# A third raw weight buffer, alternating channel groups and an earlier first norm in a one-core SSM and feed-forward kernel

## The chip, the cores and the metric

The kernel runs on one core of one Trainium2 chip. The metric is the device time of one execution in microseconds (us); a profiled execution also has a span, from its first to its last instruction. TensorE (PE) multiplies matrices into PSUM, VectorE (DVE) and ScalarE (ACT) do elementwise work, GpSimd (POOL) does some elementwise work and issues transfers, SyncE (SP) only issues transfers. Each engine takes its instructions in order.

## The reference

One layer: an adaptive layer norm, a state-space convolution over 2048 positions, a second adaptive norm and a dense feed-forward part. All is float32. Cut to what matters:

```python
mod = (silu(c) @ w_mod).reshape(1, 6, 1, 576)
sa, ca, ga, sb, cb, gb = (mod[:, i] for i in range(6))

def ssm(h):                                   # h: 2048 x 576 channels
    dt = exp(log_dt); A = -exp(log_A_real) + 1j * A_imag        # 576 x 128
    C = (C_real + 1j * C_imag) * dt[:, None]
    K = 2 * einsum("dn,dnl->dl", C, exp((A * dt[:, None])[:, :, None] * arange(2048))).real
    return causal_convolution(h, K) + h * D_skip   # in the reference by FFTs of length 4096

h = layernorm(x) * (1 + ca) + sa
x = x + ga * ssm(h)
h = layernorm(x) * (1 + cb) + sb
out = x + gb * (relu(h @ w1) @ w2)            # w1: 576 x 4608, w2: 4608 x 576
```

## The kernel before

The 2048 positions are four blocks of 512. For each block the kernel makes a convolution (`conv`, with s the block) and a feed-forward part (`ffn`). The matrix products of the feed-forward part have their operands split into a high and a low part in a faster float format (`fp32r`), and three of the four partial products are summed.

**The convolution kernel.** `KGen` builds K from powers: for each of 12 groups of 48 channels (h = 0 to 11) a table `W2` of 32 powers and a table `W1` of 16 start values, so that one small matmul gives values of K. Part of it is made at the start (`first`), and the rest later (`rest`), from tables kept in DRAM. `rest` takes a plan: for each h, which blocks of K are to be made. `load0` loads `W0` and `Z`, `load2` loads `W2`, all on POOL's queue in program order. `rots` turns `W0` by multiplying it with `Z` (four VectorE steps a rotation, lines 464 to 470) into a tile `W1r`, `products` does 96 small matmuls for each half of the group (line 498) and copies the result with ScalarE (line 508) into `ker`; after h = 5 and h = 11 it is stored to DRAM (`kd`). `spread` hands out the rotations of a group between the products of the group before. In block 0 the groups 0 to 5 make three blocks of K (three rotations, 48 columns) and 6 to 11 make one (one rotation, 16 columns).

**The convolution of a block.** `norm1` makes the first norm: eight `bn_stats`, four means and scales (`norms`), and eight VectorE operations into h (lines 914 and 915). A DFT matmul (`transform`, line 831, with ScalarE's evacuation at line 832) is made of h (`mm_U`) and of K (`mm_K`, from a tile `kt` loaded from `kd`), each in two halves p = 0, 1. `spec_U` and `spec_K` finish the spectra on VectorE by butterflies (lines 843 to 859), `product` multiplies and sums spectra of all block pairs (lines 1011 to 1017), `inverse` goes back (line 1038). Then the second norm follows, and five transposes, which give `xh`, `xl` and `xs`, the input of the feed-forward part.

**The feed-forward part.** `ffn` runs over 144 groups g, 36 for each block. A group has 14 matmuls of `first` (line 1311) into `hps`, ScalarE's `hh` (line 1316) and VectorE's `hl` (line 1317), and 14 matmuls of `second` (line 1337) into five accumulators. Its weights come by SyncE as raw tiles `r1` (line 1256) and `r2` (line 1260). ScalarE makes the high parts (`hi1`, line 1276, and `hi2`, line 1286) and in block 0 VectorE makes the low parts (`lo1`, line 1281, and `lo2`, lines 1292 and 1293), which are stored and loaded again in later blocks. There are two `r1` and two `r2` buffers; the loads at the top of group g are those of `r1[g+3]` and `r2[g+2]`.

**The order of the work.** The feed-forward part of block b is laced with the other work of the next block: `gens[b]` is a generator whose yields are costs (a number: so many us of VectorE work; None: a piece of TensorE work; -1: stop this step). `step` is called four times a group and draws from it while the work done is below a target, at most 7.5 units of VectorE work in four steps in block 0, and two pieces of TensorE work in a step. What is left after the 36th group is drained at once. For block 0 the generator is `block0`: `rest` for all 12 groups, then `conv(1)`. A scheduler places the instructions on each engine's queue, earlier program order first, as its own clock finds them ready; what goes through `Kept` stays in program order on its engine. A tile whose slot is still read waits for its readers. All transforms share one PSUM tile (`cps`).

Of the kernel before, what the change touches and what calls it, by code (L numbers as in the profile page):

```python
# [10 lines left out]
F32 = mybir.dt.float32  # L11
# [38 lines left out]
class KGen:  # L50
# [385 lines left out]
    def rest(self, psum, plan):  # L436

        nc, k = self.nc, self.k
        v = nc.vector.tensor_tensor
        hs = list(plan)  # L440
        with ExitStack() as ctx:
            pt = k.pool(ctx, f"kr{len(hs)}", side="right")
            most = used = 16 * max(len(b) for b in plan.values())

            d = Kept(k.tc, nc.gpsimd).dma_start

            def load0(h):
                W0 = pt.tile([P, 16, 2, H], F32, tag="W0", bufs=3, name=f"W0_{h}")
                Z = pt.tile([P, 2, 2, H], F32, tag="Z", bufs=3, name=f"Zr_{h}")
                d(out=W0.rearrange("p a r c -> p (a r c)"), in_=k.W1d[h])  # L450
                d(out=Z.rearrange("p i r c -> p (i r c)"), in_=k.Zd[h])
                return W0, Z

            def load2(h):
                W2 = pt.tile([P, 2, 32, H], F32, tag="W2", bufs=2, name=f"W2r_{h}")
                d(out=W2.rearrange("p r b c -> p (r b c)"), in_=k.W2d[h])
                return W2

            def rot(out, X, Z, i):
                cb = [P, 32, H]  # L460
                flat = "p a r c -> p (a r) c"
                T = pt.tile([P, 16, 2, H], F32, tag="T", name="T")
                zr, zi = (Z[:, i, r].unsqueeze(1).broadcast_to(cb) for r in range(2))
                v(T.rearrange(flat), X.rearrange(flat), zi, op=ALU.mult)
                yield 1.75
                v(out.rearrange(flat), X.rearrange(flat), zr, op=ALU.mult)
                yield 1.75
                v(out[:, :, 0], out[:, :, 0], T[:, :, 1], op=ALU.subtract)
                yield 0.95
                v(out[:, :, 1], out[:, :, 1], T[:, :, 0], op=ALU.add)  # L470
                yield 0.95

            def rots(h, W1, W0, Z):
                blocks = plan[h]
                a = [W1[:, 16 * i : 16 * i + 16] for i in range(len(blocks))]
                if blocks[0] == 1:
                    yield from rot(a[0], W0, Z, 0)
                    if len(blocks) > 1:
                        yield from rot(a[1], W0, Z, 1)
                        yield from rot(a[2], a[0], Z, 1)  # L480
                else:
                    yield from rot(a[0], W0, Z, 1)
                    yield from rot(a[1], a[0], Z, 0)

            ke = {}

            def products(h, W1, W2):
                blocks = plan[h]
                na = 16 * len(blocks)
                if h % 6 == 0:  # L490
                    ke[h // 6] = pt.tile([P, na, 72], F32, tag=f"ke{na}", bufs=1, name=f"ker_{h}")
                for half in range(2):
                    ps = psum.tile([P, 6, na], F32, tag="cps", bufs=1, name="kps")
                    for q in range(6):
                        for dd in range(4):
                            ch = dd * 12 + 6 * half + q
                            for r in range(2):
                                nc.tensor.matmul(  # L498
                                    ps[32 * dd : 32 * dd + 32, q, :],
                                    W2[:, r, :, ch],  # L500
                                    W1[:, :, r, ch],
                                    start=(r == 0),
                                    stop=(r == 1),
                                )
                        if q == 2:
                            yield None
                    q0 = 12 * (h % 6) + 6 * half
                    nc.scalar.activation(
                        ke[h // 6][:, :, q0 : q0 + 6], ps.rearrange("p q a -> p a q"), AF.Copy
                    )  # L510
                    yield None
                if h % 6 == 5:
                    yield -1
                    for i, s in enumerate(blocks):
                        self.store(
                            s, h // 6, ke[h // 6][:, 16 * i : 16 * i + 16].rearrange("p a q -> p (a q)"),
                            nc.sync,
                        )

            nxt = [load0(hs[0])]  # L520
            W2 = load2(hs[0])
            nxt.append(load0(hs[1]))
            yield -1
            prev = iter(())
            for i, h in enumerate(hs):
                W0, Z = nxt.pop(0)
                if i + 2 < len(hs):
                    nxt.append(load0(hs[i + 2]))
                na = 16 * len(plan[h])
                if used + na > most:  # L530
                    all1 = pt.tile([P, most, 2, H], F32, tag="W1", bufs=2, name=f"W1r_{h}")
                    used = 0
                W1 = all1[:, used : used + na]
                used += na
                yield from spread(rots(h, W1, W0, Z), prev, len(plan[h]))
                prev = products(h, W1, W2)
                if i + 1 < len(hs):
                    W2 = load2(hs[i + 1])
            yield from prev
# [11 lines left out]
class Body:  # L551
# [195 lines left out]
    def main(self, ctx, kg, hooks):  # L747
# [10 lines left out]

        def block0():
            self.x2p.append(self.pool(ctx, "x2b"))  # L760
            yield from kg.rest(
                self.cps, {h: (1, 2, 3) if h < 6 else (1,) for h in (6, 0, 7, 1, 8, 2, 9, 3, 10, 4, 5, 11)}
            )
            self.xp.append(self.pool(ctx, "xb"))
            pool(1)
            yield from self.conv(1)

# [134 lines left out]
    def norm1(self, x2, h):  # L902
# [9 lines left out]
        for i in range(4):  # L912
# [2 lines left out]
            f(h[:, i], h[:, i], mv[:, 3:4], self.m["sa"], op0=ALU.mult, op1=ALU.add)  # L915
            yield 1.6

    def conv(self, s):

        nc = self.nc  # L920
        v = self.vec.tensor_tensor
        xp = self.xp[s % 2]
        if s:
            x2 = self.x2p[s % 2].tile([P, 4, D], F32, tag="x2", bufs=1, name=f"x2_{s}")
            self.x2[s] = x2
            Kept(self.tc, nc.gpsimd).dma_start(
                out=x2,
                in_=self.I["x"][s * 512 : (s + 1) * 512, :].rearrange("(m n) d -> m n d", n=4),
            )
        else:  # L930
            x2, h = self.x2[0], self.h0
            self.fcKn, self.gcn = (
                self.cv.tile([P, 4, P], F32, name=n) for n in ("fcKn", "gcn")
            )
            for t, a in zip((self.fcKn, self.gcn), self.I["neg"]):
                nc.gpsimd.dma_start(out=t, in_=a)
# [4 lines left out]

        kt = [kernel_tile(0) if s else self.kt0, None]
        yield -1 if s else "mod"
        if s:
            h = self.spec(f"h_{s}").rearrange("p a b c -> p a (b c)")
        hv = h.rearrange("m n (dd p q) -> m n dd p q", dd=4, p=2)

        def mm_U(p, Z):
# [97 lines left out]
        def back(p, Y):  # L1046
            V = self.spec(f"V_{s}_{p}")
            yield from self.butterfly1(Y, V) if s == 0 and p == 0 else self.butterfly(Y, V, 1)
            Vs.append(V)
# [4 lines left out]
        if s == 0:  # L1054
# [15 lines left out]
            ZK = self.spec("Z")  # L1070
            yield from mm_K(1, ZK)
            self.save(self.Rd[0][0], Ks[0], Kept(self.tc, nc.gpsimd))
        else:
            yield from both(self.norm1(x2, h), mm_K(0, ZK))
            kt[1] = kernel_tile(1)
            ZU = self.spec("Z")
            yield from both(spec_K(0, ZK), mm_U(0, ZU))
# [19 lines left out]
        else:  # L1097
# [2 lines left out]
            Y = self.spec(f"Y_{s}_1")  # L1100
            yield from product(1, Y)
        yield from back(1, Y)
        xh = xp.tile([P, 4, 512], F32R, tag="xh", bufs=1, name=f"xh_{s}")
        xl = xp.tile([P, 4, 512], F32R, tag="xl", bufs=1, name=f"xl_{s}")
        xs = xp.tile([P, 512], F32R, tag="xs", bufs=1, name=f"xs_{s}")
# [138 lines left out]
    def ffn(self, gens):  # L1244
# [11 lines left out]
            queue(g).dma_start(out=r1[g], in_=I["w1"][g % NF])  # L1256

        def load_r2(g):
            r2[g] = ff.tile([P, D], F32, tag="r2", bufs=2, name="r2")
            queue(g + 1).dma_start(out=r2[g], in_=I["w2"][(g % NF) * P : (g % NF) * P + P, :])  # L1260

        def low1(g):
# [118 lines left out]
        yield  # L1381
        load_r2(1)
        load_r1(2)
        prev = None
        for g in range(n + 1):
            if g < n:
                if g + 3 < n:
                    load_r1(g + 3)
                if g + 2 < n:
                    load_r2(g + 2)  # L1390
                for dst, src in late:
                    nc.sync.dma_start(out=dst, in_=src.bitcast(F32))
                late.clear()
# [74 lines left out]
def both(a, b):  # L1468

    while True:  # L1470
        n = 0
        for g in (a, b):
            for w in g:
                n = 1
                yield w
                break
        if not n:
            return
# [62 lines left out]
```

## Time and profile before

| what | us |
|---|---|
| median of three runs | 1353.58 |
| lowest and highest run | 1346.75, 1354.69 |
| the profiled execution, own time | 1347.4 |
| its span | 1345.6 |
| feed-forward block 0 (first group to first group) | 221.6 to 554.1 |
| block 1 | 554.1 to 844 |
| blocks 2 and 3 and the end | 844 to 1345.6 |

The rows quoted below come from the profiled execution. L12 is line 12 of the kernel; "out<-in" names the tiles of an instruction; a wait names the engine and line that ended it. PEld is TensorE's loading of weights, SPq and POOLq are the queues that issue transfers. PEclk is the share of TensorE's full clock that was granted. In the chain of waits each row is a start, a duration, and what the time went to.

### The profile page before, as it was taken

The numbers are of one execution on the slowest core, as the hardware profiler recorded it, in microseconds if no ns is written. First come the engines' busy times: TensorE is split into PE (matmuls) and PEld (weight loads), VectorE is DVE, ScalarE is ACT, GpSimd is POOL, SyncE is SP. The second block draws the span as 40 slices with busy tenths as digits, with TensorE's granted clock in tenths as the row PEclk, the third lists the DMA queues.
The fourth block names the chain that finished last, engine by engine and source line by source line (L and its number), as shares of the span: only waits on it lengthen the run. The fifth ranks groups of instructions, "written<-read, shape, count | busy, mean of one in ns | idle before, by whom it ended". The sixth has DMA issues, their size and how long they took to land.

```text
span 1345.6 us, 26013 instructions
## 1 busy us (share of the span) xinstructions
PE 1232.3 (92%) x10720; PEld 983.7 (73%) x10720; DVE 892.2 (66%) x1324; ACT 496.4 (37%) x863; POOL 162.4 (12%) x260
## 2 busy tenths in 40 slices
PE   4556686999999898999999999999999999999997
PEld 2344565778777686777777887887888888888885
DVE  5989978999986899588458985467996221111112
ACT  5778423222224322622244225433323352323331
POOL 0657411001000000100001000100000000000000
PEclk9658887999999999999999999999999999999998
DMA  8567975788867866898778995877996567666661
GB/s 269 217 240 287 332 269 182 283 306 304 302 237 264 332 224 259 262 409 285 244 275 328 343 364 162 271 223 269 348 393 189 176 178 230 194 196 198 199 186 53
DMA packets 120843, 345.85 MB, mean 257 GB/s; under 512 B 23916, under 2 KB 24212, under 8 KB 109972
## 3 DMA queue, kind: packets, MB, share of 16 engines
q1 hardware_dynamic: 103828, 226.96, 51.2%
q0 software_dynamic: 16384, 115.85, 22.7%
q8 instruction: 84, 1.38, 0.4%
q10 hardware_dynamic: 512, 1.38, 0.4%
q14 instruction: 35, 0.29, 0.1%
HBM read 262.73 MB, written 81.40 MB: 256 GB/s over the span
## 4 chain that ended last, share of the span: by engine, by line
PE 82%; DVE 8%; DMA 4%; issue 3%; ACT 2%; POOL 1%; POOLq 0%; ACTq 0%; SPq 0%; DVEq 0%
PE acc L1337 33%; PE hps L1311 33%; PE kps L498 5%; PE ps_f L831 5%; PE kps L71 2%; PE ps_i L1038 2%; DMA r<-in_w_dram 2%; PE ph L71 1%; DMA Zr<-Zd 1%; DVE T L62 1%; DVE W L62 1%; DVE k L62 1%; PE ps_t L1133 0%; POOL W L68 0%; DMA kt<-kd 0%
## 5 line engine op out<-in xcount | busy, mean ns | idle before, releaser
L1311 PE MATMUL hps<-xh,w 128*128 128x512 f32 x1152 | 394.0, 401 | 0.7 <-ACT xh L47 0.7
L1337 PE MATMUL acc<-w,hh 128*128 128x512 f32 x1152 | 369.3, 401 | 4.2 <-ACT hh L1316 4.2
L1317 DVE SCALAR_TENSOR_TENSOR hl<-hps,hh 128x512 fp32r<-128x512 f32 x144 | 99.0, 688 | 324.5 <-ACT hh L1316 323.8
L1337 PEld LDWEIGHTS acc<-w,hh 128*128 128x128 f32 x1152 | 215.7, 188 | 51.0 <-ACT hh L1316 4.6
L1311 PEld LDWEIGHTS hps<-xh,w 128*128 128x128 f32 x1152 | 216.9, 189 | 48.4 <-ACT xh L47 1.3
L1311 PE MATMUL hps<-xl,w 128*128 128x512 f32 x576 | 230.1, 400 | 0.1
L1337 PE MATMUL acc<-w,hl 128*128 128x512 f32 x576 | 223.2, 399 | 1.3 <-DVE hl L1317 1.3
L1316 ACT ACTIVATE hh<-hps 128x512 fp32r<-128x512 f32 x144 | 86.1, 598 | 303.3 <-PE hps L1311 301.6
L1286 ACT ACTIVATE w<-r 128x576 fp32r<-128x576 f32 x141 | 96.8, 686 | 268.6 <-PE acc L1337 197.3
L1337 PEld LDWEIGHTS acc<-w,hl 128*128 128x128 f32 x576 | 108.0, 188 | 25.6 <-DVE hl L1317 2.5
L1311 PEld LDWEIGHTS hps<-xl,w 128*128 128x128 f32 x576 | 108.7, 189 | 23.9 <-DVE xl L47 0.8
L1276 ACT ACTIVATE w<-r 128x640 fp32r<-128x640 f32 x140 | 102.5, 732 | 24.7 <-DMA r<-in_w_dram 23.3
L1311 PE MATMUL hps<-xs,w 128*128 128x512 f32 x288 | 96.6, 407 | 0.0
L498 PEld LDWEIGHTS kps<-W1r,W2r 128*32 128x32 f32 x3456 | 67.8, 146 | 30.5 <-issue 19.8
L71 PE MATMUL kps<-W,W 128*32 128x16 f32 x2304 | 45.1, 217 | 44.6 <-POOL W L68 29.0
L498 PE MATMUL kps<-W1r,W2r 128*32 128x16 f32 (+2 forms) x3456 | 76.4, 238 | 7.3 <-issue 4.7
L71 PEld LDWEIGHTS kps<-W,W 128*32 128x32 f32 x2304 | 40.4, 150 | 55.7 <-POOL W L68 31.4
L1017 DVE TENSOR_TENSOR Y<-Y,T 128x1152 f32<-128x1152 f32 x60 | 79.3, 1349 | 0.0
L832 ACT ACTIVATE Z<-ps_f 128x288 f32<-128x288 f32 x120 | 48.9, 409 | 69.5 <-PE ps_f L831 68.3
L1455 POOL DMA_DIRECT2D out_dram<-x x16 | 8.7, 545 | 467.0 <-DVE x L1447 464.7
L1311 PEld LDWEIGHTS hps<-xs,w 128*128 128x128 f32 x288 | 53.4, 189 | 11.6 <-DVE xs L1142 0.3
L1337 PE MATMUL acc<-hl,w 128*128 128x512 f32 x144 | 56.9, 395 | 0.0
(230 smaller groups left out, 1565.4 us busy)
## 6 DMA issues: line engine op xcount, KB each, us to landing
r<-in_w_dram SPq DMA_DIRECT2D x144, 320.0 KB, 3.9
r<-in_w_dram SPq DMA_DIRECT2D x144, 288.0 KB, 4.6
w<-L1d SPq DMA_DIRECT2D x108, 320.0 KB, 4.8
w<-L2d SPq DMA_DIRECT2D x108, 288.0 KB, 2.7
W2r<-W2d POOLq DMA_DIRECT2D x18, 1536.0 KB, 8.8
W2d<-W SPq DMA_DIRECT2D x12, 1536.0 KB, 8.6
Ua<-Ud POOLq DMA_DIRECT2D x15, 1152.0 KB, 9.4
W<-W1d POOLq DMA_DIRECT2D x18, 768.0 KB, 10.1
```

What stands on the lines that cost most here:

```text
L62: self.tc.keep_in_program_order(self.nc.vector.tensor_tensor(out, a, b, op=op))
L71: self.tc.keep_in_program_order(self.nc.tensor.matmul(*args, **kw))
L498: nc.tensor.matmul(ps[32 * dd : 32 * dd + 32, q, :], W2[:, r, :, ch], W1[:, :, r, ch], start=(r == 0), stop=(r == 1),)
L831: nc.tensor.matmul(o, fc[:, n2, c, :], src(n2), start=True, stop=True)
L832: ev = nc.scalar.activation(Z[:, n2, c], ps[:, :PC], AF.Copy)
L1017: v(y, y, T, op=op or ALU.add)
L1276: copy(g - 1)(w1[g][:, 0], r1[g], AF.Copy)
L1286: copy(g)(w[:, 0:D], r2[g], AF.Copy)
L1311: nc.tensor.matmul(ps, a, x, start=(i == 0), stop=(i == 13))
L1316: nc.scalar.activation(hh, ps, AF.Relu)
L1317: nc.vector.scalar_tensor_tensor(hl, ps, 0.0, hh, op0=ALU.max, op1=ALU.subtract)
L1337: nc.tensor.matmul(acc[i], a, x, start=(f == 0 and seen[i] == 1), stop=(f == NF - 1 and seen[i] == (3 if i < 4 else 2)),)
```

## The change

Three things are changed.

- `r2` gets a third buffer; the load at the top of group g becomes `r2[g+3]`, and `r2[2]` is loaded ahead of the loop.
- In `rest` the tiles `W1r` were parts of two slots of 48 columns' size. Now there is one slot for each size where the sizes alternate, and two where they don't (block 1). The order of the 12 groups in block 0 becomes 0, 6, 1, 7, 2, 8, 3, 9, 4, 10, 5, 11; it was 6, 0, 7, 1, 8, 2, 9, 3, 10, 4, 5, 11.
- The load of the next block's `x` and `norm1` become a generator `head`. In block 0 it starts at group 5, and one piece of it follows each TensorE piece of `rest`. Its result lies in a pool `hp` of its own, which is closed before the pool `xb` for `xh`, `xl` and `xs` is opened; `xb` is opened at the end of the convolution, where it was opened ahead of it. With h ready, `conv(1)` begins with the transform of U in place of that of K. For blocks 2 and 3 `head` is drawn from inside `conv`, at the places where its parts stood.

```diff
@@ rest
-            most = used = 16 * max(len(b) for b in plan.values())
...
             for i, h in enumerate(hs):
+                if len(hs) == NH and h == 5:
+                    yield "head"
                 W0, Z = nxt.pop(0)
                 if i + 2 < len(hs):
                     nxt.append(load0(hs[i + 2]))
                 na = 16 * len(plan[h])
-                if used + na > most:
-                    all1 = pt.tile([P, most, 2, H], F32, tag="W1", bufs=2, name=f"W1r_{h}")
-                    used = 0
-                W1 = all1[:, used : used + na]
-                used += na
+                bufs = 1 if len(plan[h]) != len(plan[hs[i - 1]]) else 2
+                W1 = pt.tile([P, na, 2, H], F32, tag=f"W1{na}", bufs=bufs, name=f"W1r_{h}")
@@ block0
-            yield from kg.rest(
-                self.cps, {h: (1, 2, 3) if h < 6 else (1,) for h in (6, 0, 7, 1, 8, 2, 9, 3, 10, 4, 5, 11)}
-            )
-            self.xp.append(self.pool(ctx, "xb"))
+            hp = ExitStack()
+            self.hp = self.pool(hp, "hp")
+            plan = {h: (1, 2, 3) if h < 6 else (1,) for h in (0, 6, 1, 7, 2, 8, 3, 9, 4, 10, 5, 11)}
+            head = iter(())
+            for w in kg.rest(self.cps, plan):
+                if w == "head":
+                    head = self.head(1)
+                    continue
+                yield w
+                if w is None:
+                    for x in head:
+                        yield x
+                        break
+            yield from head
+
+            def xb():
+                hp.close()
+                self.xp.append(self.pool(ctx, "xb"))
+
+            self.xb = xb
@@ Body
+    def head(self, s):
+
+        x2 = self.x2p[s % 2].tile([P, 4, D], F32, tag="x2", bufs=1, name=f"x2_{s}")
+        self.x2[s] = x2
+        Kept(self.tc, self.nc.gpsimd).dma_start(
+            out=x2,
+            in_=self.I["x"][s * 512 : (s + 1) * 512, :].rearrange("(m n) d -> m n d", n=4),
+        )
+        yield 0.0
+        if s == 1:
+            self.h1 = self.hp.tile([P, 4, D], F32, name="h_1")
+        else:
+            self.h1 = self.spec(f"h_{s}").rearrange("p a b c -> p a (b c)")
+        yield from self.norm1(x2, self.h1)
@@ conv
+        if s > 1:
+            norm = self.head(s)
+            next(norm)
...
         yield -1 if s else "mod"
+        if s > 1:
+            first_part = next(norm)
...
+        elif s == 1:
+            ZU = self.spec("Z")
+            yield from mm_U(0, ZU)
+            yield from both(spec_U(0, ZU), mm_K(0, ZK))
+            kt[1] = kernel_tile(1)
+            Z1 = self.spec("Z")
+            yield from both(spec_K(0, ZK), mm_U(1, Z1))
+            ZK = self.spec("Z")
+            first[0] = self.load(self.Ud[0][0], "Ua")
+            yield from both(spec_U(1, Z1), mm_K(1, ZK))
         else:
-            yield from both(self.norm1(x2, h), mm_K(0, ZK))
+            yield first_part
+            yield from both(norm, mm_K(0, ZK))
             kt[1] = kernel_tile(1)
             ZU = self.spec("Z")
             yield from both(spec_K(0, ZK), mm_U(0, ZU))
...
         yield from back(1, Y)
+        if s == 1:
+            self.xb()
+        xp = self.xp[s % 2]
@@ ffn
-            r2[g] = ff.tile([P, D], F32, tag="r2", bufs=2, name="r2")
+            r2[g] = ff.tile([P, D], F32, tag="r2", bufs=3, name="r2")
...
         load_r1(2)
+        load_r2(2)
...
-                if g + 2 < n:
-                    load_r2(g + 2)
+                if g + 3 < n:
+                    load_r2(g + 3)
```

More of the change, by code (lines that the diff above doesn't have):

```diff
@@ L921, in conv @@
         v = self.vec.tensor_tensor
-        xp = self.xp[s % 2]
+        if s > 1:
+            norm = self.head(s)
+            next(norm)
         if s:
[L924 to L929, printed above, removed]
+            x2 = self.x2[s]
         else:
@@ L943, in conv @@
         yield -1 if s else "mod"
+        if s > 1:
+            first_part = next(norm)
         if s:
-            h = self.spec(f"h_{s}").rearrange("p a b c -> p a (b c)")
+            h = self.h1
         hv = h.rearrange("m n (dd p q) -> m n dd p q", dd=4, p=2)
```

## The prediction

> **What bounds the kernel now.** I read the page first: the busy shares, then the chain that ended last.
>
> ```profile
> span 1345.6 us, 26013 instructions
> PE 1232.3 (92%) x10720; PEld 983.7 (73%) x10720; DVE 892.2 (66%) x1324; ACT 496.4 (37%) x863; POOL 162.4 (12%) x260
> PE 82%; DVE 8%; DMA 4%; issue 3%; ACT 2%; POOL 1%; POOLq 0%; ACTq 0%; SPq 0%; DVEq 0%
> ```
>
> TensorE carries 82% of the chain. The share is a mean over unlike stages, so the second view is the table of engines by stretch. I cut it where the work of feed-forward block 0 changes: the channel groups of `rest`, their end, the four transforms of the next convolution, its products and inverses; then block 1, then blocks 2 and 3.
>
> ```profile
> core 0: us, PE busy (x) PEld busy (x) DVE busy (x) ACT busy (x) POOL busy (x), PEclk, DMA share, GB/s
> 221.60:390.50 168.90, 163.32 (x2413) 130.12 (x2414) 160.72 (x171) 44.53 (x79) 18.33 (x35) 0.99 0.83 297
> 390.50:425.30 34.80, 34.80 (x498) 28.47 (x496) 17.27 (x42) 9.71 (x20) 1.72 (x2) 1.00 0.82 295
> 425.30:474.10 48.80, 45.05 (x177) 31.98 (x176) 41.81 (x64) 20.72 (x45) 4.93 (x8) 0.97 0.75 271
> 474.10:554.10 80.00, 75.62 (x323) 60.13 (x321) 72.89 (x119) 26.31 (x45) 2.65 (x5) 0.98 0.73 256
> 554.10:844.00 289.90, 286.97 (x2295) 228.04 (x2295) 210.09 (x267) 103.65 (x191) 24.88 (x43) 1.00 0.82 295
> 844.00:1345.00 501.00, 491.70 (x2172) 402.95 (x2170) 201.53 (x287) 164.72 (x281) 16.69 (x30) 0.99 0.69 221
> ```
>
> Two engines are full in block 0: VectorE is busy 160.7 of 168.9 us in the first stretch and 72.9 of 80.0 in the fourth, and TensorE is nearly full too. Only the second stretch is unlike the rest: VectorE works half of it, yet TensorE works all 34.8 us. From 554 us on TensorE is busy 98 to 99% of the time; nothing of this change can win much there. One feed-forward group costs TensorE 28 matmuls:
>
> ```profile
> 412.45 3.17 PE hps L1311 x14
> 415.62 3.17 PE acc L1337 x14
> ```
>
> so 6.34 us is a group's floor. The third view is what TensorE waited for within block 0 (221 to 554 us; line, releaser, total, times, longest; two waits under 1 us follow), the stock from which this change can gain:
>
> ```profile
> PE acc L1337 <- ACT hh L1316: 4.2, 1, 4.2
> PE ps_f L831 <- ACT Z L832: 3.7, 1, 3.7
> PE kps L498 <- issue: 2.9, 2, 1.9
> PE kps L498 <- ACT ker L508: 2.6, 1, 2.6
> ```
>
> That is 13.4 us. Two of the waits are long, and each is followed by a dip of the granted clock (0.97 and 0.98 in their stretches, 1.00 before): 0.03 of 48.8 us and 0.02 of 80.0 us, about 1.5 us apiece. Stock in all: 16.4 us.
>
> **The change part by part.**
>
> *The norm moves into the last channel groups.* Eight statistics and eight scalings leave the head of the convolution.
>
> ```profile
> 402.45 2.97 DVE L880 BATCH_NORM_STATS2 st<-x 128x6 f32<-128x288 f32 x8
> 410.00 0.69 DVE L1317 SCALAR_TENSOR_TENSOR hl<-hps,hh 128x512 fp32r<-128x512 f32 x1 [3.11 <-ACT hh L1316]
> 416.35 0.69 DVE L1317 SCALAR_TENSOR_TENSOR hl<-hps,hh 128x512 fp32r<-128x512 f32 x1 [3.84 <-ACT hh L1316]
> 422.63 0.69 DVE L1317 SCALAR_TENSOR_TENSOR hl<-hps,hh 128x512 fp32r<-128x512 f32 x1 [3.72 <-ACT hh L1316]
> 424.00 1.54 DVE L914 SCALAR_TENSOR_TENSOR h<-x,mv,m_ca 128x576 f32<-128x576 f32 x2
> 425.46 1.54 DVE L915 SCALAR_TENSOR_TENSOR h<-h,mv,m_sa 128x576 f32<-128x576 f32 x2
> ```
>
> The statistics ran in VectorE's slack already. The scalings are two pairs of rows like the last two, 4 x 1.5 = 6 us, and they start at 424.0, after 10.7 us in which VectorE idled and TensorE did not. The obvious hope, 10.7 us, is therefore not to be had: TensorE ran at its floor right there. What moving 6 us away can do is relieve the stretch behind it. There the chain shows this:
>
> ```profile
> 450.25 0.75 DVE w L1281
> 450.99 0.02 issue
> 451.01 7.94 DMA r<-in_w_dram
> ```
>
> Line 1281 is the last reader of a raw `w1` tile; it stood behind a run of butterflies on VectorE, so the reload of that tile (line 1256) went out at 451.01 and landed 7.9 us later; ScalarE, in order, waited for it with an evacuation (line 832) behind, and TensorE waited 3.7 us for that. With 6 us less queued on VectorE line 1281 comes earlier by more than the 3.7 us. I take the wait and its dip as gone: -3.7 - 1.5 = -5.2 us; the ends are 0 and -5.2.
>
> The Trainium skill's page "TensorE: Matmul & The Clock Gate", Part 1, says the clock falls to half after about one idle window of 3.4 us and comes back after one busy window. By that rule each of the two long waits would cost 1.7 us more, instead of the 1.5 I took from the clock column; the sum would be -5.4 in place of -5.2.
>
> The moved norm also takes its `x` load with it, on POOL's queue one group earlier, ahead of the weights of group 11; a load that VectorE now meets inside a full stretch. The issues of raw weights, `x` and `kt` (KB each, median us to landing), and two of the rotations' four steps:
>
> ```profile
> r<-in_w_dram SPq DMA_DIRECT2D x144, 320.0 KB, 3.9
> r<-in_w_dram SPq DMA_DIRECT2D x144, 288.0 KB, 4.6
> x<-in_x_dram POOLq DMA_DIRECT2D x3, 1152.0 KB, 9.2
> kt<-kd POOLq DMA_DIRECT2D x6, 576.0 KB, 8.3
> ```
>
> ```profile
> L464 DVE TENSOR_TENSOR T<-W,Zr 128x1536 f32<-128x1536 f32 x24 | 42.0, 1750 | 8.8 <-DMA Zr<-Zd 8.8
> L468 DVE TENSOR_TENSOR W1r<-W1r,T 128x768 f32<-128x768 f32 x36 | 34.2, 950 | 0.2
> ```
>
> The handing-out puts the first statistic three of group 5's twelve rotation steps behind the load: one of 1.75 and two of 0.95 us, 3.7 us. If it is queued there, VectorE stands up to 9.2 - 3.7 = 5.5 us with group 11's rotations and the `hl` of a group behind it, and TensorE behind those. But 6 us and more of idle VectorE follow, so I take +1, nearer to the slack; ends 0 and +5.5.
>
> *Alternation.* Each group of `rest` already got a tile of its own out of two slots, so group i+2 waited for the products of group i; with one slot for each of the two sizes it still does. Same instructions, same waits (lines 466 on 498). What differs is the order. Group 0 with three rotations now comes first instead of group 6 with one; TensorE gets its first products three rotations later and does feed-forward groups meanwhile. The 2.6 us wait on line 508 lay at these first products, behind a raw load on ScalarE. I take -1.8 of it; ends -2.6 and, if TensorE meets the longer rotation at its first product instead, +2.4, one more wait as long as the longest that VectorE has there:
>
> ```profile
> DVE W1r L466 <- PE kps L498: 6.8, 4, 2.4
> SPq L1260 <- DVE w L1293: 192.6, 29, 15.4
> ACT w L1286 <- DMA r<-in_w_dram: 55.2, 11, 10.0
> ACT w L1276 <- DMA r<-in_w_dram: 20.7, 10, 9.4
> ```
>
> *The third `r2` buffer.* The reload at line 1260 waits for line 1293 (192.6 us in all, SyncE's own idle time). With three buffers the tile loaded in group g still goes into the one that group g's low part has read, so it is issued at the same moment; it only lands one group ahead of need. ScalarE's 55.2 us before line 1286 would go. But line 1276, the raw `w1` with its two buffers as before, is right behind: of the other long wait the chain shows
>
> ```profile
> 507.14 13.03 DMA r<-in_w_dram
> ```
>
> that is `w1` again, landing after 13.0 us where the median is 3.9 to 4.6. The 4.2 us wait on line 1316 lies behind it on ScalarE; so it stays, and I take 0 for the buffer; ends 0 and -5.7 (4.2 and its dip).
>
> *The new order of transforms* (U first, kernel second) is the same 32 transforms of one PSUM tile: cost 0, as long as the second `kt` load stays hidden (rival two).
>
> *The count of steps.* By the handing-out rule (at most 7.5 units of VectorE work in four steps, two pieces of TensorE work in each) I counted the yields of both versions: the generator of block 0 is empty in group 34 before and in group 33 after. Nothing is left over for the drain in either; no term.
>
> Sum: -5.2 + 1 - 1.8 = -6.0 us. The profiled execution took 1347.4 us (span 1345.6), 6 us under the median of the three runs, 1353.58, near the lowest, 1346.75. A difference carries over: 1353.6 - 6.0 = 1347.6 us.
>
> **The rivals.** *One: the whole stock goes.* If less pressure on VectorE brings line 1281 forward everywhere and early `w2` loads free ScalarE, all 16.4 us of the stock fall: 1337.2. For it: both long waits are a raw tile reloaded late. Against: the second lies 90 us behind the norm, amid the transfers of the products, which stay. Chance 0.24.
>
> *Two: slower, by the second kernel tile.* `kt` has one buffer. Before, its reload had two phases (norm or K beside U) before its reader came; now the kernel transform is second and only one phase of eight transforms lies between.
>
> ```profile
> 429.29 0.48 PE ps_f L831 x2
> 430.48 0.55 PE ps_f L831 x2
> 435.25 1.17 POOL L1234 DMA_DIRECT2D kt<-kd  x1 [30.08 <-DMA r<-in_w_dram]
> POOL Rd L822 <- DVE K L859: 17.5, 2, 14.0
> ```
>
> Eight transforms at 1.2 us are 10 us of cover; the load needs 1.2 to issue and 8.3 to land. It decides from half a us on: if POOL, in order, first waits for VectorE to finish a tile that it stores (14.0 us the longest), the load lands up to 14 us late, TensorE stands in order with the feed-forward matmuls behind it, and the clock dips: +14 + 1.5 - 6.0 = +9.5, 1363; without the other gains +15.5, 1369. Against: loads and stores are not kept in program order there, so POOL may take the load first. Chance 0.18. The page "DMA: Bandwidth & Descriptors" of the Trainium skill puts the fixed cost of a transfer at about 2 us; by it this load would be hidden; the 8.3 us row says that under this traffic it lands four times later.
>
> *Three: nothing moves.* The third buffer is issued by the same event, and the late `w1` only shows up at another group: 1353.6. Chance 0.18.
>
> **How the numbers follow.** The forecast has 0.40. About 1% (13.5 us) is what a measurement of this kernel can tell from no change: its three runs lie 0.6% apart. Faster by more needs rival one: 0.24. Slower by more needs rival two without the other gains: 0.12, the rest of its 0.18 lies within. Within 1%: 0.64. The range reaches from 1332, which lies between rival one reckoned from the median (1337) and from the lowest run (1346.75 - 16.4 = 1330), to the middle between rival two's two ends, 1366.
>
> **What would show it.** Right: the scalings of the norm lie before the last products of `rest`, the stretch after them has no wait of TensorE over 3 us at line 831 and a clock of 1.00; the idle time of line 1286 on raw loads falls by most of 55 us while that of line 1276 stays or grows; blocks 1 to 3 are as they were. Wrong: a wait of TensorE or VectorE on `kt` or `x`, or new waits of ScalarE on `w1` loads in front of line 832 or 1316; or a first feed-forward block shorter by over 15 us, which would mean that the late reloads were VectorE's doing throughout.

## The result and the profile after

| | median of 20 runs, us | lowest, highest |
|---|---|---|
| before | 1348.66 | 1346.02, 1354.69 |
| changed | 1350.14 | 1346.08, 1354.43 |

The ratio of changed to before is 1.0004, with a 95% interval from 0.9993 to 1.0016. That is no change: at most 1 us gained or 2 us lost. The forecast was 1347.6 from a base of 1353.58, a ratio of 0.9956, and 0.9956 lies outside the interval. So the time is within the stated range and within 1%, as the likeliest class had it, but the small gain of 6 us is not there. That the forecast in us is only 2.5 us off is luck: the base of three runs was itself 5 us high (over 20 runs the kernel before has 1348.66), and that hides most of the gain that did not come.

In the changed kernel line 1352 is the old 1311 (`hps`), 1378 is 1337 (`acc`), 1357 is 1316 (`hh`), 1317 and 1327 are 1276 and 1286 (the high parts of `w1` and `w2`), 1322 is 1281 (low part of `w1`), 844 and 845 are 831 and 832 (transform and evacuation). The table of engines by stretch of the changed kernel, cut at the first matmul of groups 0, 18, 26, 36 and 72 (columns as in the prediction's table):

```profile
223.30:393.40 170.10, 163.85 (x2413) 128.88 (x2414) 156.81 (x169) 44.97 (x79) 18.54 (x35) 0.99 0.82 295
393.40:471.90 78.50, 78.50 (x672) 59.18 (x671) 63.52 (x108) 30.19 (x65) 6.66 (x10) 1.00 0.83 303
471.90:554.20 82.30, 76.66 (x330) 60.54 (x329) 72.42 (x120) 28.52 (x49) 2.66 (x5) 0.98 0.72 250
554.20:844.50 290.30, 288.03 (x2289) 228.77 (x2288) 209.66 (x266) 101.69 (x187) 24.89 (x43) 0.99 0.83 294
```

and of the kernel before at the same groups, where the prediction's table was cut elsewhere:

```profile
390.50:474.10 83.60, 79.85 (x672) 60.44 (x671) 59.08 (x105) 30.43 (x65) 6.65 (x10) 0.98 0.78 281
554.10:844.10 290.00, 287.07 (x2295) 228.14 (x2295) 210.09 (x267) 103.65 (x191) 24.88 (x43) 1.00 0.82 295
```

Stretch by stretch: the channel groups 170.1 against 168.9 (+1.2), the transforms 78.5 against 83.6 (-5.1), products and inverses 82.3 against 80.0 (+2.3), block 1 +0.3. The sum is -1.3, of a profile whose span is 0.7 us longer in all, 1346.3 us; the part ahead of block 0 was 1.7 us longer in this execution, and the end 0.3. So something was won in the place that the prediction named, and most of it was lost on both sides of it.

TensorE's waits in block 0 of the changed kernel (line, releaser, total, times, longest; five shorter rows follow):

```profile
PE acc L1378 <- ACT hh L1357: 8.0, 3, 4.3
PE hps L1352 <- ACT xh L47: 1.2, 1, 1.2
PE hps L1352 <- DVE w L1322: 1.1, 1, 1.1
PE kps L496 <- PE hps L1352: 1.0, 1, 1.0
```

The 3.7 us wait at the evacuation is gone, and the transforms run at a full granted clock, 1.00 where it was 0.98. In its place there are two more waits at `hh`: 8.0 us in three, where there had been 4.2 in one. All TensorE's waits in block 0 add up to 13.8 us where they had been 14.3. ScalarE's waits for raw tiles show what the third `r2` buffer did:

```profile
ACT w L1317 <- DMA r<-in_w_dram: 55.7, 16, 8.4
ACT w L1327 <- DMA r<-in_w_dram: 0.3, 1, 0.3
```

The wait of 55.2 us at the high part of `w2` is now 0.3, but the one at `w1`, 20.7 before, has become 55.7. ScalarE takes both in order: of 76 us of waiting 56 are left, and they stand one instruction further on.

### The profile page after: what moved, and what is told of

Read it like the earlier page. It is cut to its first block, busy times and chain, and to the rows that moved or that the text cites. A ratio compares the mean times of both kernels' runs of the same rounds, so it can differ in the third digit from the quotient of the medians.

```text
span 1346.3 us, 26017 instructions
## 1 busy us (share of the span) xinstructions
PE 1236.1 (92%) x10720; PEld 983.0 (73%) x10720; DVE 892.7 (66%) x1324; ACT 496.9 (37%) x863; POOL 162.5 (12%) x260
## 4 chain that ended last, share of the span: by engine, by line
PE 82%; DVE 10%; DMA 3%; issue 2%; ACT 1%; POOL 1%; POOLq 0%; ACTq 0%; SPq 0%; DVEq 0%
PE acc L1378 32%; PE hps L1352 32%; PE kps L496 5%; PE ps_f L844 5%; PE kps L71 2%; PE ps_i L1065 2%; PE ph L71 2%; DMA r<-in_w_dram 2%; DVE W1r L464 1%; DVE T L62 1%; DVE T L462 1%; DMA Zr<-Zd 1%; DVE k L62 1%; PE ps_t L1174 1%; POOL W L68 1%
## 5 line engine op out<-in xcount | busy, mean ns | idle before, releaser
L1352 PE MATMUL hps<-xh,w 128*128 128x512 f32 x1152 | 388.2, 397 | 1.2 <-ACT xh L47 1.2
L496 PE MATMUL kps<-W1r,W2r 128*32 128x48 f32 (+2 forms) x3456 | 76.3, 238 | 1.9 <-PE hps L1352 1.0
```

The costliest lines, as they stand in the source:

```text
L496: nc.tensor.matmul(ps[32 * dd : 32 * dd + 32, q, :], W2[:, r, :, ch], W1[:, :, r, ch], start=(r == 0), stop=(r == 1),)
L1352: nc.tensor.matmul(ps, a, x, start=(i == 0), stop=(i == 13))
```

## The experiments

Each is timed in five rounds beside the kernel before on the same chip, and the ratio is to that kernel; the runs were spread over three chips. The short names are those of the expectations. In runs built on the kernel before the lines have other numbers again: 1306 is `hps`, 1311 `hh`, 1332 `acc`, 826 and 827 transform and evacuation, 1271 the high part of `w1`; with both raw buffers 1313 is `hh`, 1314 `hl`, 1334 `acc` and 1273 the high part of `w1`.

**The order alone.** The kernel before with only this:

```diff
-    for h in (6, 0, 7, 1, 8, 2, 9, 3, 10, 4, 5, 11)
+    for h in (0, 6, 1, 7, 2, 8, 3, 9, 4, 10, 5, 11)
-    all1 = pt.tile([P, most, 2, H], F32, tag="W1", bufs=2, name=f"W1r_{h}")
+    W1 = pt.tile([P, na, 2, H], F32, tag=f"W1{na}", bufs=bufs, name=f"W1r_{h}")
```

> The kernel before with the alternating order and the tiles by size alone (two r2 buffers, the norm in its old place, K first). Theory A (the long waits of TensorE are reloads of raw w1 tiles that go out late; the order moves the first of them, the moved norm took away the one in the transforms, nothing else mattered): the wait in the transforms of about 3.7 us stays as before, the start of block 0 is about 1 us longer as in the changed kernel, ratio 1.001 (0.999 to 1.004). Rival B (the alternation itself costs what the norm's move gains, some 4 us): ratio 1.003 or more.

> The order alone once more, since its cost rests on six runs: 1.003 to 1.006 if the order costs what it showed; 0.999 to 1.002 if those runs were unlucky, and then the moved norm gained nothing either.

Measured: 1.0044 (1.0028 to 1.0060), and in the repeat 1.0030 (1.0015 to 1.0045). The order costs 4 to 6 us. The first is Rival B's number and not Theory A's; the repeat lies where the two ranges overlap, and its interval lies above 1 too. Rows of the table by stretch, the channel groups of the first run, then the channel groups and the products of the second:

```profile
225.50:395.70 170.20, 165.34 (x2412) 131.32 (x2413) 159.44 (x170) 44.82 (x79) 18.49 (x35) 0.98 0.81 292
```

```profile
221.70:392.50 170.80, 166.15 (x2413) 131.98 (x2414) 159.95 (x170) 44.12 (x79) 18.49 (x35) 0.97 0.81 291
477.10:558.10 81.00, 76.20 (x323) 60.88 (x322) 73.03 (x119) 26.19 (x45) 2.65 (x5) 0.96 0.73 251
```

The reader is to see TensorE's busy time and the clock: the same 2412 or 2413 matmuls are busy 165.3 and 166.2 us where they were 163.3, and the granted clock is 0.98 and 0.97 for 0.99. In the third stretch it is 0.96 for 0.98. So much of the loss is no idle time at all, but slower matmuls behind the waits. The waits of the second of these runs:

```profile
PE acc L1332 <- ACT hh L1311: 6.8, 3, 4.4
PE ps_f L826 <- ACT Z L827: 3.3, 1, 3.3
PE kps L496 <- issue: 3.1, 2, 2.1
```

With the small ones they add up to no more than before (14.3 us both; in the first run 16.1), but there are three at `hh` instead of one. In the two profiles the clock records show half speed for 13.7 and 17.1 us in block 0, where the kernel before has 6.8 (a dip that lies across the beginning of the block in all three is left out); half of the difference, 3.4 and 5.1 us, is time lost, about the whole price. Of the added dips one lies at 246 us in the first run and two at 243 and 267 us in the second, early in the channel groups, where the kernel before has none; and the dip in the products, 3.4 us long before, is 6.8 in both. By stretch the order alone is longer than before by 1.3 and 1.9 us in the channel groups, 1.4 and 1.0 in the transforms, 0.6 and 1.0 in the products, 0.5 and 0.3 in block 1: 3.8 and 4.2 in all.

The Trainium skill's page "TensorE: Matmul & The Clock Gate", Part 1, says that the clock drops to half after an idle window of 3.4 us, and that the window runs freely. The length agrees: each dip in block 0 is 3.4 us or twice that. But a wait need not fill a window here. In the second run TensorE waited 2.0 us at 240.4, was busy 1.4 of the 3.4 us ahead of 242.6, and the clock dipped there; in the changed kernel a wait of 2.1 us at the same point, 241.9, was followed by no dip, nor was the one of 2.6 us in the kernel before. So which short wait costs a dip as well is partly luck, and waits of equal sum need not cost equal time.

**The small group first.** The same with the order 6, 0, 7, 1, 8, 2, 9, 3, 10, 4, 11, 5, alone and in the changed kernel (where the norm then starts at group 11).

> The kernel before with strict alternation that begins with the small group (6, 0, 7, 1, ... 4, 11, 5) and tiles by size. Theory F (the order alone cost 4 to 8 us because the group of three rotations comes first: TensorE gets no products before group 3, two waits at hh follow): with the small group first the ratio is back at 0.998 to 1.002, products begin in group 2. Rival G (the cost lies at the end of the channel groups or in the tiles by size, not at the beginning): ratio 1.003 to 1.006 as with the large group first.

> The changed kernel with its alternation turned to begin with the small group and to end with a large one (6, 0, ... 4, 11, 5); the norm starts at group 11, again the last but one. Theory F: the moved norm keeps its gain of about 6 us (first to eighth group behind the channel groups 78 us against 83.6 before) and the order costs nothing, ratio 0.994 to 0.997. Rival G: ratio 0.999 to 1.002 as the changed kernel.

Measured: 1.0010 (0.9991 to 1.0028) alone, and 0.9988 (0.9968 to 1.0009) in the changed kernel. Alone it is Theory F's number, and it lies under both runs that began with the large group, although its interval overlaps that of the second. In the changed kernel it is neither: better than 1.0004 by an amount that the intervals don't separate, and not the 0.994 to 0.997 that Theory F gave. This points to the large group at the beginning for most of the order's cost; the two gains don't simply add. (In the one profiled execution of the changed kernel with the small group first, 2 us slower than the median of its runs, no gain is to be seen: the four stretches take 622.9 us against 621.2.)

The clock records of all 14 profiles bear it out. In each of the nine with the large group first a dip of 3.4 us or more begins between 242 and 272 us; in the five that begin with a small group, the kernel before among them, none begins there. The small group first has one wait at `hh` again, 4.1 us in the products, and its first two stretches together take 252.9 us, where the kernel before has 252.5 and the order alone 255.2 and 255.4.

**Without the third `r2` buffer.** The changed kernel with

```diff
-            r2[g] = ff.tile([P, D], F32, tag="r2", bufs=3, name="r2")
+            r2[g] = ff.tile([P, D], F32, tag="r2", bufs=2, name="r2")
-        load_r2(2)
-                if g + 3 < n:
-                    load_r2(g + 3)
+                if g + 2 < n:
+                    load_r2(g + 2)
```

> The changed kernel with two r2 buffers again. Theory A (the third r2 buffer is issued by the same event and only moves ScalarE's idle time from the high part of w2 to that of w1): ratio as the changed kernel, 1.000 (0.998 to 1.003); in block 0 ScalarE idles over 40 us before the high part of w2 on raw loads and under 25 us before that of w1; TensorE has the same waits of 2 to 4.5 us at hh. Rival B (the buffer was worth something that another part gave back): ratio 1.003 or more above the kernel before.

Measured: 0.9998 (0.9985 to 1.0011), the time of the changed kernel. ScalarE waits at the high part of `w2` again, with the rows as expected:

```profile
ACT w L1327 <- DMA r<-in_w_dram: 72.1, 15, 10.0
ACT w L1317 <- DMA r<-in_w_dram: 24.0, 10, 8.2
```

Together 96 us, against 56 with the buffer; and 40 us less of ScalarE's waiting is worth nothing in time. This run is also the order and the moved norm together: against the order alone, the norm (with U ahead of K) gains 0.3 to 0.5%, 4 to 6 us. Its transforms take 77.7 us and its products 83.3:

```profile
393.00:470.70 77.70, 77.70 (x672) 59.26 (x671) 62.64 (x107) 30.29 (x65) 6.64 (x10) 1.00 0.86 314
470.70:554.00 83.30, 77.68 (x330) 60.94 (x329) 73.13 (x121) 28.45 (x49) 2.64 (x5) 0.96 0.68 239
```

**The third `r2` buffer without the norm.** The order with the buffer, the norm in its old place.

> The kernel before with the changed order and a third r2 buffer alone. The buffer is worth nothing without the moved norm too: ratio 1.003 to 1.006 as the order alone; ScalarE's wait moves from the high part of w2 to that of w1. If it is worth something alone: 1.001 or less.

Measured: 1.0014 (0.9998 to 1.0029), between the two answers; the intervals don't decide whether it is worth something alone. The trace does say what it does: the wait at the evacuation is gone here too, and the transforms take 80.4 us where the order alone has 85.0 and 84.6. The reload of raw `w1` behind which that wait lay goes out 10.2 us after the first matmul of group 22; in the kernel before and with the order alone it is 25.8 us.

```profile
391.70:472.10 80.40, 78.82 (x672) 59.49 (x671) 58.73 (x104) 30.56 (x65) 6.11 (x9) 1.00 0.79 289
```

**The third buffer for `r1`.** In the changed kernel in place of the one for `r2`, and on the order alone:

```diff
-            r1[g] = ff.tile([P, 5, P], F32, tag="r1", bufs=2, name="r1")
+            r1[g] = ff.tile([P, 5, P], F32, tag="r1", bufs=3, name="r1")
```

> The changed kernel with the third buffer given to r1 in place of r2. Theory A (raw w1 is what is late): the reload is no longer held by the low part on VectorE, it goes out a group earlier; TensorE's 8.0 us of waits on ScalarE's hh in block 0 fall to under 3 us with the dips of the clock behind them, ratio 0.993 to 0.997. Rival C (the DMA queues are full there, an earlier issue lands no earlier): the waits stay within 2 us of 8 and the ratio within 0.998 to 1.002. Rival D (VectorE's backlog takes over): waits on hh fall but those on hl rise by as much, ratio 0.998 to 1.002.

> The kernel before with the alternating order and a third r1 buffer, the norm in its old place. Theory A: the wait in the transforms goes without the norm's move, since its cause was the reload of raw w1; ratio 0.993 to 0.997, within 0.002 of the run with the norm moved. Rival E (the norm's move is what took it, by VectorE's load): the 3.7 us wait in the transforms stays and the ratio is 0.003 above that run.

Measured: 0.9997 (0.9982 to 1.0012) with the norm moved, a miss for Theory A; its waits at `hh` fell to 3.6 us, but 4.3 us on `hl` came instead, Rival D. On the order alone 0.9982 (0.9969 to 0.9996): a gain of 0.5 to 0.6% over the order alone, though less than Theory A's 0.993 to 0.997, and the transforms at 78.6 us without the norm's move, against Rival E:

```profile
392.80:471.40 78.60, 78.60 (x672) 58.95 (x671) 59.35 (x106) 29.34 (x64) 6.63 (x10) 1.00 0.80 294
```

So the wait in the transforms goes by any one of three edits: the norm moved away, a third `r1` buffer, a third `r2` buffer. Whoever makes two of them wins it once.

**The order of the transforms.** The changed kernel with K first again:

```diff
-            yield from mm_U(0, ZU)
-            yield from both(spec_U(0, ZU), mm_K(0, ZK))
+            yield from mm_K(0, ZK)
             kt[1] = kernel_tile(1)
...
+            yield from both(spec_K(0, ZK), mm_U(0, ZU))
```

> The changed kernel with the transform of K first again and then that of U, as before; the norm stays moved. If the gain in the transforms comes from VectorE's relief alone (the step of the prediction): groups 18 to 25 take 78 to 79 us as in the changed kernel, ratio 0.999 to 1.002. If it comes from the order of transforms (U needs no kernel tile and can begin early): they take 82 us or more and the ratio is 1.003 to 1.005.

Measured: 0.9997 (0.9977 to 1.0016), and 79.0 us for the transforms: U first is not needed for the gain. But this run has the third `r2` buffer, which by itself takes the wait away with K first (80.4 us). With two buffers the norm was moved only with U first. That VectorE's relief alone would do it, in the old order of the transforms, is argued and not shown.

**Both raw buffers.** The order, three buffers each for `r1` and `r2`, the norm in its old place, with the large group first and with the small one. Room comes from the pool of `xh`, `xl`, `xs` opened late, two buffers for T and, in block 1, two for W0.

> The kernel before with the changed order and three buffers each for r1 and r2; to make room, the pool of xh, xl and xs is opened at the end of the convolution, the temporary T of the products has two buffers and W0 in block 1 two. Theory A (a late raw tile is behind the waits at hh; with one of the two at two buffers that one becomes the late one): ScalarE's idle time on raw loads in block 0 falls under 20 us in sum where it was 74 us, waits at hh under 2 us, ratio 0.993 to 0.997. Rival C (DMA traffic): idle time on raw loads stays over 40 us. Rival D (VectorE's backlog): waits at hl over 4 us in place of hh, ratio 0.997 to 1.000.

> The order with both raw buffers and without the moved norm, begun by the small group. Theory F (the first group costs about 4 us): ratio 0.990 to 0.993, 0.003 under the same kernel with the large group first. If the third raw buffers already hide what the first group cost: 0.994 to 0.997.

Measured: 0.9954 (0.9932 to 0.9975) and 0.9961 (0.9945 to 0.9978). Both beat the kernel before and the changed one, by 5 to 7 us, and what the first group cost shows no more. (The three edits that make room were not tried alone.) Of the first, in a profiled execution that was the slowest of its runs, 7 us above their median:

```profile
ACT w L1273 <- DMA r<-in_w_dram: 28.2, 6, 11.0
```

```profile
PE acc L1334 <- ACT hh L1313: 3.1, 2, 2.6
PE acc L1334 <- DVE hl L1314: 1.0, 1, 1.0
```

ScalarE's waits for raw tiles are down to 28 us from 76 and those at `hh` to 3.1: not the under 20 and under 2 expected, but Theory A's number in time, and neither Rival C nor D.

**All together.** The changed kernel with both raw buffers and the small group first. The room for it took a buffer from Z as well, and the tile `cb` is made twice.

> The changed kernel with three buffers for r1 as well as r2 and the alternation begun by the small group; room for it: two buffers for Z and for the temporary T of the products, two for W0 in block 1, and the small tile cb made twice. If late raw tiles and the first group are what is left: waits at hh under 4 us in block 0, ratio 0.988 to 0.994, below that of the order with both raw buffers and without the moved norm (0.995). If the moved norm and the raw buffers win the same time twice (both took the wait out of the transforms): ratio 0.994 to 0.997, no better than that run.

Measured: 1.0034 (1.0017 to 1.0051), slower, against both answers. Its waits at `hh` are 1.7 us, as expected, but the channel groups now take 180.0 us:

```profile
225.10:405.10 180.00, 171.06 (x2603) 134.99 (x2604) 165.53 (x181) 45.16 (x82) 18.48 (x35) 0.98 0.78 282
```

```profile
PE kps L496 <- issue: 7.3, 5, 2.4
```

This stretch holds 190 matmuls of `rest` more than that of the changed kernel, because the small group comes first; the next stretch has as many less. The changed kernel with the small group first has them too and takes 174.8 us, so 5.2 us are new, and its waits of this kind are 1.3 us against the 7.3 here. The likely cause is Z with two buffers: POOL's loads of Z wait 102 us for VectorE in this stretch, where they wait 23 in the other run. It was not tried apart, so the run doesn't tell what norm and both buffers would give with room to spare.

## Why the prediction was right in size and wrong in its sum

*The moved norm: -5.2 us, right.* The transforms became 5.1 us shorter, the 3.7 us wait and the dip of the clock went. (The dip is 3.4 us at half speed in the records, so 1.7 us lost, and not 1.5.) The path is as predicted: with the norm moved and two `r2` buffers the reload of raw `w1` goes out 9.8 us after the first matmul of group 22, where it was 25.8 us. How much of this the new order of transforms gives is open. Not all scalings made it into the channel groups: the last four instructions begin at 412.5 us, the last product of `rest` at 409.7; this cost nothing that shows. The 10.7 us of VectorE's idle time ahead of it were worth nothing, as argued: TensorE was full there before (34.8 of 34.8 us).

*Its echo, not foreseen: +2.3 us.* With the norm moved, the stretch of products and inverses takes 82.3, 83.3 and 83.5 us (changed; without the buffer; K first) where the order alone has 80.6 and 81.0. The prediction took what is won in a stretch to be won for good. Of the 2.3 us 1.0 is TensorE's busy time: 16 transposes of the second norm lie ahead of the cut instead of 8. The waits in the stretch are 5.6 us instead of 4.4; 1.1 of it is a new wait of line 1352 for the low part of `w1`, line 1322 on VectorE. Block 1, with eight transposes less, still became no shorter (+0.3): it has a dip of the clock, 3.4 us at 581 us, that it did not have before. What sets that new wait isn't settled.

*The `x` load: +1 us, not to be seen.* VectorE met it inside a full stretch, as predicted, and waited 2.7 us:

```profile
DVE st L893 <- DMA x<-in_x_dram: 2.7, 1, 2.7
```

But the channel groups are no longer for it: 170.1, 170.0 and 169.3 us with the norm moved (changed; without the buffer; K first), 170.2 and 170.8 with the order alone.

*The alternation: -1.8 us, the step that failed.* The prediction saw only that the 2.6 us wait at the first products would move, took 1.8 us of it as won without a row for that size, and bounded the cost at +2.4 by one more wait of VectorE. The order alone cost 4 to 6 us. The 2.6 us wait did not go, it changed its place. TensorE's first product of `rest` comes at 250.1 us, where it came at 235.2. The wait lay behind a raw `w1` tile that ScalarE waited for until 241.7 us; in the changed kernel ScalarE waits for it until 242.2, and TensorE, which has no products yet, waits 2.1 us at `hh`:

```profile
241.69 0.74 ACT L1276 ACTIVATE w<-r 128x640 fp32r<-128x640 f32 x1 [9.38 <-DMA r<-in_w_dram]
```

```profile
242.18 0.74 ACT L1317 ACTIVATE w<-r 128x640 fp32r<-128x640 f32 x1 [8.19 <-DMA r<-in_w_dram]
```

A second wait at `hh` came on top, 1.6 us at 251.2. The clock dips behind it or, with the order alone, behind the first, so that the cost is more than the waits' length. The chain of the changed kernel shows where the second comes from:

```profile
240.76 0.74 DVE w L47 x2
241.49 0.75 DVE w L1322
242.24 0.02 issue
242.26 9.17 DMA r<-in_w_dram
```

```profile
251.54 0.60 issue
252.14 0.59 ACT hh L1357
252.73 0.04 issue
252.77 0.82 PE acc L1378 x2
```

It is the same loop as in the transforms: line 1322 late on VectorE, which now has three rotations at the very beginning, the reload of raw `w1` behind it, 9.2 us to land, ScalarE in order, TensorE behind `hh`. The prediction knew this loop and did not ask what the new order would do to it.

*The third `r2` buffer: 0, right on top of the norm,* and by the reason given: it moves ScalarE's wait to `w1`, and the long wait in the products stays. What the prediction did not see is that the buffer alone also takes away the wait in the transforms, which it had given to the norm.

*The rivals.* The second kernel tile never came late. The store ahead of it on POOL was through 5 us earlier, and the reload went out as soon as its last reader was done:

```profile
437.90 0.54 POOL L835 DMA_DIRECT2D Ud<-U  x1 [27.18 <-DVE U L872]
443.10 1.17 POOL L1275 DMA_DIRECT2D kt<-kd  x1 [4.67 <-PE ps_f L844]
```

Rival three, nothing moves, had the time but only half of the reason: the late `w1` did show up at other groups, but the transforms' wait was truly gone. So signs of both kinds came that the prediction had named: those of its being right at lines 831, 1286 and 1276, and two of its being wrong, VectorE's wait on `x` and a new wait of ScalarE on `w1` ahead of `hh`. The other long wait, behind a reload of `w1` amid the products' transfers, stayed as said; the reload took 11.9 us where it had taken 13.0. By the runs the order costs 4 to 6 us, the norm on top of it gains 4 to 6, the buffer on top of both nothing: the change as a whole is +0.5 us, between -1 and +2.

## What to carry to other kernels

When several edits aim at the same wait, price them as one: here a moved norm, a third `r1` and a third `r2` buffer each remove the same 3.7 us, and only once. Where one engine takes two streams in order, a buffer for one of them can move the wait to the other, as the one for `r2` did; here the one for `r1` won 0.5 to 0.6% over the order alone, both together 0.8 to 0.9%. A reordering of equal work is not free because its waits look the same: where it puts the longest piece of work at a point at which a reload hangs on the same engine, it makes new waits, and here a wait of 2 us could cost 1.7 us more by a dip of the clock behind it.

## What the runs showed of the hardware

The time ahead of the feed-forward part varied by 6 us between profiles, from 221.3 to 227.4, and by 3.8 us between two profiles of the same kernel, the order alone. The half-speed records in it add up to 109 and 95 us in the two that were through earliest, and to 126 and 123 us in the two that were latest. This goes with the 8 us over which the runs of one kernel spread; whether the clock is its cause or its effect no run shows. And a transfer's landing depends on company: the raw `w1` tile lands in 3.6 to 7.4 us in the median of a kernel, but in 7.9 to 13.3 us at the points where it decided.

The Trainium skill's page "DMA: Bandwidth & Descriptors" (section "Anatomy of one DMA") puts the fixed cost of a transfer that GpSimd issues at about 2 us and adds the bytes at 436 GB/s. By it the 576 KB of a kernel tile `kt` would take about 3.4 us, an estimate; the prediction had set its 8.3 us beside the fixed part alone. The two such loads for block 1 in the changed kernel landed after 7.4 and 7.6 us, over twice the estimate.
